# Retention and an exact-GELU MLP on one core: q and k turned as 2-byte values, one plane per feature of a pair

## The chip, the core and the metric

The kernel runs on one core of a Trainium2 chip. A core has TensorE (PE in the profile: matrix products; PEld is its weight load), VectorE (DVE), ScalarE (ACT), GpSimd (POOL), SyncE (SP) and 16 DMA engines. The metric is the device time of one execution in microseconds, the median of several runs. Inputs and the output are float32; the products inside run in bfloat16.

## The reference

```python
# q, k, v: (8 batches, 8 heads, 576 positions, 64 features)
scores = scale * np.matmul(q, k.transpose(0, 1, 3, 2))
gamma = 1.0 - 2.0 ** (-5.0 - np.arange(H, dtype=np.float32))
rel = pos[:, None] - pos[None, :]
Dmat = np.where(rel >= 0, gamma[:, None, None] ** rel[None, :, :], 0.0)
ret = scores * Dmat[None, :, :, :]
attn = np.matmul(ret, v)
# x: (4608 tokens, 512)
x = attn.transpose(0, 2, 1, 3).reshape(B * S, H * D)
h = x @ w_in                    # w_in: (512, 2048)
g = 0.5 * h * (1.0 + erf(h * inv_sqrt2))
out = g @ w_out                 # w_out: (2048, 512)
```

There is no softmax: scores are multiplied by a power of gamma that depends on the distance. That lets the sum over distant keys be kept as a state of 64 x 64 per head, so that only a block of 128 x 128 around the diagonal needs explicit scores.

## The kernel before

**Units and groups.** A unit is 128 positions of one batch, with all eight heads. The first four units are position block 0 of batches 0 to 3, each a group by itself ("raw" units). After them come groups of two units (two batches, the same block of positions); the last 64 positions of two batches form one short unit, a group of one. For a group the steps are: turn q and k so that features lie on partitions (T), scores (S, function `scores`), mask and copy out of PSUM (`masked`, line 628), product with v (`inner`), the state (`state`), the product of q with the state (`cross`), and the evacuation into x (`evacuate`, line 771). Four units fill one block of 512 tokens of x, of which there are nine; a block then goes through the MLP: `mlp1` or `mlp1_fast` with `w_in`, GELU on ScalarE, `mlp2` or `mlp2_fast` with `w_out`. The fast forms compute a product of 2 x 2 blocks with seven block products, for which VectorE makes sums of operands.

**How q and k are turned.** There are three ways. Units 0 to 3 and the two groups after them (`BY_PE`) are transposed by TensorE and copied out of PSUM. The other 16 groups (`BY_DVE`) are turned by VectorE, which transposes blocks of 32 x 32. For these, the load puts the data so that 32 partitions hold 32 blocks of t consecutive positions (t = 4 for a full unit, 2 for a short one), and each quarter of the partitions holds one combination of head parity and batch. A head has 64 features but a quarter has 32 partitions, so each partition holds two adjacent features, a pair. In the kernel before, `turn_dve` (line 550) reads the 2-byte data as 4-byte values, one value per pair, and so keeps the two features of a pair side by side. For k the products read the result with a step of two. For q a function `apart` (line 561) copies it on ScalarE into two halves, one for each feature of the pair, back into q's load buffer. Scores and `cross` run one product for each feature of the pair and add them up.

**Buffers.** Tiles are taken in rings with a tag: "lq" and "lk" hold loaded q and k, "tq" and "tk" turned ones, "kn" k in its plain layout, "v" and "vh" v and v scaled. A ring's tile is taken again once a condition given with it holds; `nT`, `nA` and `nB` count the groups turned and the units whose scores and whose product with v have been put out.

**The order of work.** All instructions are put out by a planner written in Python, which runs when the kernel is built. It keeps a clock `T` for each engine, adds a fixed duration to it for each instruction, notes when each load should land (`land`), and at each step of TensorE's clock picks what is due (the loop from line 1274). `fire` (line 1193) puts out the side work of the other engines. `AHEAD` and `RATE` bound how far the scores may run ahead of the MLP; `LEAD` says from which lead on two neighbouring groups do their products with v and the state together, `NEAR` how long MLP work holds back for that, `JOIN` allows scores right behind such a step. The order in which GpSimd puts out the first loads is a list, `ORDER`: q, k, v with the number of a unit, "wi" and "wo" eighths of `w_in` and `w_out`, "n" a plain copy of k, "dq" a step of the table of decays, and "io" the constants (line 187), which begin with two index ramps on GpSimd (lines 188 and 190); the identity for TensorE's transposes and the decay masks `near` follow from them on VectorE and ScalarE. Unit 0's q, k and v are loaded by SP's and ScalarE's queues as float32 and cast.

**Warm-up and fill.** TensorE begins with `N_WARM` products of 512 columns on a tile of zeros. Later, up to `WARM_TO`, the planner puts such products into gaps that it foresees (`warm`, line 1230). `HOT` is the time until which it counts a product at twice its duration.

The lines that turn and copy q, before:

```python
src = loaded[groups[n][0]][0][x][:, 0:2 * m].bitcast(FP32).rearrange("p (h t e) -> p h t e", h=HP, e=32)
dst = (turned(n, 1) if x else sg[n]["pairs"]).rearrange("p h s -> p (h s)")[:, 0:2 * m].bitcast(FP32)
nc.vector.transpose(dst.rearrange("p (h b t) -> p h t b", h=HP, b=32), src)
```

Of the kernel before, what the change touches and what calls it, by code (L numbers as in the profile page):

```python
# [9 lines left out]
FP32 = mybir.dt.float32  # L10
BF16 = mybir.dt.bfloat16
# [6 lines left out]
def kernel(  # L18
# [54 lines left out]
    BY_PE = range(4, 4 + NPE)  # L73
    BY_DVE = range(4 + NPE, N_G)
    raw = range(4)
    N_LQ = 6
    N_LK = 4
    N_TQ = 2
    N_TK = 4
    N_KN = 4  # L80
    VH_POOL = 16
    N_VH = 4
    VH_ACT = [4, 22, 1]
    N_XB = 4
    AHEAD = 13
    RATE = 4.6
    STORE_AT = 62.0
    CROWD = 66.0
    STATE10 = 32.0
    HOT = 7.5  # L90
    FETCH = 5.0
    ARRIVE = 5.6
    WPLUS = 0
    WARM_TO = 24.0
    JOIN = 0
    JOIN_SB = 0.0
    VISIT = 4
    LEAD = 5.0
    NEAR = 0.6
    SLACK, SB, PER_G, PER_B, TURN0 = 1.2, 2.0, 8.0, 20.0, 0.0  # L100
    FINE = 0.38
    FPOOL = 0.6
    N_V = 6
    MASK_ACT = 99.0
    V0_HW = 1
    N_WARM = 7
    MSK_AT = 24.0
    HK = N_DF // 2

    const = ctx.enter_context(tc.tile_pool(name="const", bufs=1))  # L110
# [156 lines left out]
    def tiles_of(i):  # L267
        g = groups[group_of[i]]
        if i not in loaded:
            if i < 4:  # L270
                loaded[i] = ([early_slice(2 * i + a, 1).rearrange("p (h d) -> p h d", h=H) for a in range(2)],
                             early_slice(8 + i, 1).rearrange("p (h d) -> p h d", h=H), None)
            else:
                n = group_of[i]
                if i != g[0]:
                    qk, v_, kn = loaded[i - 1]
                elif n in BY_PE:
                    qk = [ring("lq", [128, 2 * H * D], BF16, "q_ld", lambda: nB > g[-1]),
                          ring("lk", [128, 2 * H * D], BF16, "k_ld", lambda: all(y in s_done for y in g) and nT > n)]
                    kn = qk[1].rearrange("p (h j d) -> p j h d", j=2, h=H)  # L280
                else:
                    qk = [ring("lq", [128, 2 * H * D], BF16, "q_ld", lambda: nB > g[-1]),
                          ring("lk", [128, 2 * H * D], BF16, "k_ld", lambda: nT > n)]
# [97 lines left out]

    def next_order():
        item = ORDER.pop(0)
# [122 lines left out]
    def turned(n, x):  # L506

        s = sg[n].setdefault("turned", {})
        if n < 4:
            if not s:  # L510
                t = ring("kn", [128, 2, HP, 128], BF16, "qkT", lambda: nB > n)
                s[0], s[1] = t[:, 0], t[:, 1]
        elif x not in s:
            s[x] = ring("tk", [128, H, 128], BF16, "kT", lambda: nA > groups[n][-1])
        return s[x]

    def turn(n, jj):

        qk = loaded[groups[n][0]][0][jj]
        if n < 4:  # L520
            b, t = bank([128, HP, 128], BF16, "qk_ps")
            dst, m = turned(n, jj), HP
            for x in range(HP):
                mm_turn(t[:, x], qk[:, 2 * x:2 * x + 2, :], ident1)
        else:
            b, t = bank([128, H, 128], BF16, "qk_ps")
            dst, m = turned(n, 1) if jj else qk.rearrange("p (h s) -> p h s", h=H), H
            for y in range(2):
                for hp in range(HP):
                    mm_turn(t[:, y * HP + hp], qk[:, 4 * D * hp + y:4 * D * hp + 4 * D:2], ident1)  # L530
# [7 lines left out]
    apart_due = []  # L538

    def pairs_of(n):  # L540
        return HP * (TAIL if units[groups[n][0]][2] is None else C)

    def turn_dve(n, x):

        m = pairs_of(n)
        src = loaded[groups[n][0]][0][x][:, 0:2 * m].bitcast(FP32).rearrange("p (h t e) -> p h t e", h=HP, e=32)
        if x == 0:
            sg[n]["pairs"] = ring("tq", [128, H, 128], BF16, "qT", lambda: n not in [x[0] for x in apart_due])
        dst = (turned(n, 1) if x else sg[n]["pairs"]).rearrange("p h s -> p (h s)")[:, 0:2 * m].bitcast(FP32)
        nc.vector.transpose(dst.rearrange("p (h b t) -> p h t b", h=HP, b=32), src)  # L550
        done = on("dve", 0.13 + m / 530, max(land["qk"[x], i] for i in groups[n])) + SEM
        if x == 0:
            apart_due.append((n, done))
        else:
            sg[n]["T"] = max(sg[n].get("T", 0.0), done)

    def apart():

        n, ready = apart_due.pop(0)
        m = pairs_of(n)  # L560
        nc.scalar.copy(loaded[groups[n][0]][0][0][:, 0:2 * m].rearrange("p (y n) -> p y n", y=2),
                       sg[n]["pairs"].rearrange("p h s -> p (h s)")[:, 0:2 * m].rearrange("p (n y) -> p y n", y=2))
        sg[n]["T"] = max(sg[n].get("T", 0.0), on("act", 0.15 + m / 580, ready) + SEM)

    def turned_q(n, sl, hp, y):
        m = pairs_of(n)
        return loaded[groups[n][0]][0][0][sl, y * m + hp * m // HP:y * m + (hp + 1) * m // HP]

    def turned_k(n, sl, hp, y):
        m = pairs_of(n)  # L570
        if n in BY_PE:
            return turned(n, 1)[sl, y * HP + hp, :]
        return turned(n, 1)[sl].rearrange("p h s -> p (h s)")[:, 2 * hp * m // HP + y:2 * (hp + 1) * m // HP:2]

    def scores(n):
        g = groups[n]
# [9 lines left out]
        else:  # L586
            short = len(g) == 1
            got = [bank_pair(TAIL if short else C) for _ in g]
            for hp in range(HP):
                for y in range(2):  # L590
                    for e in range(2):
                        for j in range(2):
                            sl = slice(64 * e + 32 * j, 64 * e + 32 * j + 32)
                            dst = got[0][1][64 * j:64 * j + 64, e, hp, :] if short else got[j][1][:, e, hp, :]
                            mm(dst, lhsT=turned_k(n, sl, hp, y), rhs=turned_q(n, sl, hp, y),
                                             start=(y == 0), stop=(y == 1), skip_group_check=True)
            done = pe(0.25 if short else 0.42, "row4x2" if short else "row4")
            for j, i in enumerate(g):
# [136 lines left out]
    def cross(n):  # L735
# [6 lines left out]
        for hp in range(HP):  # L742
            for y in range(2):
                for e in range(2):
                    for j in range(2):
                        sl = slice(64 * e + 32 * j, 64 * e + 32 * j + 32)
                        mm(o[64 * e:64 * e + 64, j, hp, :], lhsT=u[sl, 2 * hp + y, :], rhs=turned_q(n, sl, hp, y),
                                         start=False, stop=(hp == HP - 1 and y == 1), skip_group_check=True)
        done = pe(0.25 if j0 is None else 0.4, "row4x2")
        for i in g:  # L750
# [442 lines left out]
    def fire():  # L1193
# [17 lines left out]
        while apart_due and apart_due[0][1] <= now + 0.1 and T["act"] <= now + (0.5 if apart_due[0][0] > group_of[min(nA, N_U - 1)] else 3.0):  # L1211
            apart()
        while True:
            jobs = side_jobs(now)
            if not jobs:
# [39 lines left out]
    def s_ready(early=0):  # L1255
        n = group_of[nA]
        g = groups[n]
        if n < nT and n not in [x[0] for x in apart_due] and g[-1] // 4 <= tM1 + N_XB - 1 and nA + len(g) <= AHEAD + early + RATE * b1:
            return sg[n]["T"]
        return 1e9  # L1260

# [7 lines left out]
    for _ in range(N_WARM):  # L1269
        b, t = bank([128, 512], FP32, "warm")  # L1270
        mm(t, lhsT=zeros[:, :128], rhs=zeros, start=True, stop=True)
        release(b, 0.0)
    T["pe"] = 1.3 + 0.62 * N_WARM
    while True:
        fire()
        now = T["pe"]
# [97 lines left out]
        if apart_due:  # L1374
            soon.append(max(apart_due[0][1], T["act"]) + 0.01)
        if wsum or sum_due:
            soon.append(T["dve"] + 0.01)
        if stores:
# [41 lines left out]
```

## Time and profile before

| | |
|---|---|
| median of 3 runs | 292.75 us (291.52 to 293.8) |
| span of the profiled execution | 288.7 us |
| granted TensorE clock in it | 1.000 |
| instructions | 9727 |
| DMA | 31.96 MB, mean 111 GB/s |

The span reaches from the first to the last instruction of the profiled execution. Busy times of an engine are unions of its instructions' durations; products overlap in the array, so a group's mean duration is longer than its share of the time. Rows of a group read: line, engine, operation, output and inputs, shape, count, then busy us and the mean ns of one, then idle time of the engine just before, and what ended it. Rows of the timeline read: start us, us, engine, line, operation, count, and in brackets the idle time before it. Rows by stage give the stretch, its length, then for each engine its busy time and count of instructions, the granted clock, DMA and GB/s.

### The profile page before, as it was taken

Reading aid. Unit: us, or ns where it says so; the run is one execution under the profiler, and the core shown is the slowest. Engines: PE = TensorE matmul, PEld = TensorE weight load, DVE = VectorE, ACT = ScalarE, POOL = GpSimd, SP = SyncE. Lnnn points to the kernel's source line nnn. Section 1 sums busy time; section 2 is a strip of 40 time slices with the busy share of each in tenths; the row PEclk is TensorE's granted clock in tenths of the full one; section 3 lists DMA queues with packets and bytes.
Section 4 is the critical chain, followed back from the end, with each engine's and each line's share of the span. In section 5 each row is a group of like instructions: output and inputs, shape, how many; then the busy total and the mean of one; then the engine's idle time right before and its main releaser. Section 6 shows DMA issues by size and latency. Waiting matters only on the chain.

```text
span 288.7 us, 9727 instructions
## 1 busy us (share of the span) xinstructions
PE 279.1 (97%) x4138; PEld 212.5 (74%) x4162; DVE 229.5 (80%) x384; ACT 178.8 (62%) x400; POOL 136.2 (47%) x205
## 2 busy tenths in 40 slices
PE   6899999999999999999999999999999999999994
PEld 2478767888667766666766766777888888888883
DVE  5564289897964799968996799897996998899861
ACT  7355537998378767778578866655645455555421
POOL 8956868996899777678688820000000000000000
PEclk9999999999999999999999999999999999999999
DMA  9999999999989999999999960302020202101114
GB/s 155 170 183 202 185 163 203 201 124 150 116 98 135 140 169 116 184 133 190 163 122 185 82 104 3 77 2 75 0 75 0 76 3 73 73 2 73 39 55 128
DMA packets 109131, 31.96 MB, mean 111 GB/s; under 512 B 85792, under 2 KB 104736, under 8 KB 109088
## 3 DMA queue, kind: packets, MB, share of 16 engines
q0 software_dynamic: 100400, 21.12, 83.2%
q1 hardware_dynamic: 7264, 9.51, 9.9%
q10 hardware_dynamic: 1424, 0.72, 0.9%
q8 instruction: 32, 0.52, 0.7%
q14 instruction: 11, 0.09, 0.1%
HBM read 42.99 MB, written 9.44 MB: 182 GB/s over the span
## 4 chain that ended last, share of the span: by engine, by line
PE 95%; DMA 2%; issue 1%; DVE 0%; POOL 0%; ACT 0%; POOLq 0%; DVEq 0%
PE psum L452 93%; DMA early<-in_q_dram 2%; PE psum L456 1%; POOL w_in L311 0%; DVE qkT L487 0%; DVE o_sb L884 0%; ACT t L489 0%; POOL val L188 0%; POOLq L188 0%; DVEq L487 0%; POOLq L1404 0%; POOL pos L190 0%
## 5 line engine op out<-in xcount | busy, mean ns | idle before, releaser
L452 PE MATMUL psum<-x,w_in 128*128 128x256 bf16 (+2 forms) x716 | 116.8, 303 | 1.6 <-issue 0.8
L452 PEld LDWEIGHTS <-w_in 128*128 128x128 bf16 x736 | 68.1, 98 | 26.1 <-issue 0.3
L452 PEld LDWEIGHTS <-g_all 128*128 128x128 bf16 x576 | 55.6, 98 | 15.1 <-issue 0.6
L452 PE MATMUL psum<-w_out,g_all 128*128 128x256 bf16 (+1 forms) x438 | 58.6, 280 | 0.0
L799 ACT ACTIVATE g_all<-psum 128x512 bf16<-128x512 f32 x64 | 37.7, 594 | 22.8 <-PE psum L452 22.5
L452 PEld LDWEIGHTS <-s 128*128 128x128 bf16 x408 | 39.3, 98 | 8.5
L346 POOL DMA_DIRECT2D k_ld<-in_k_dram x64 | 35.1, 566 | 18.1 <-DMA q_ld<-in_q_dram 10.3
L645 ACT ACTIVATE vh<-v_ld,dv 128x128 bf16<-128x128 bf16 (+1 forms) x144 | 42.2, 379 | 0.0
L628 DVE TENSOR_TENSOR ret<-psum,msk 128x1024 bf16<-128x1024 f32 (+1 forms) x32 | 35.6, 1150 | 7.3 <-PE psum L452 7.2
L1013 ACT ACTIVATE g_all<-t 128x512 bf16<-128x512 f32 x36 | 22.6, 630 | 29.0 <-DVE t L1021 28.9
L346 POOL DMA_DIRECT2D q_ld<-in_q_dram x64 | 35.3, 570 | 2.0 <-DMA v_ld<-in_v_dram 0.9
L452 PE MATMUL psum<-wt,s 128*128 128x256 bf16 x272 | 34.3, 273 | 0.0
L489 ACT COPY t<-psum 128x256 f32<-128x256 f32 (+1 forms) x46 | 20.0, 436 | 21.8 <-PE psum L452 21.5
L884 DVE TENSOR_TENSOR o_sb<-psum,t 128x256 f32<-128x256 f32 x51 | 21.4, 420 | 12.0 <-ACT t L489 6.3
L1021 DVE TENSOR_TENSOR t<-psum,t 128x512 f32<-128x512 f32 x36 | 24.7, 689 | 6.1 <-ACT t L489 4.2
L487 DVE COPY t<-psum 128x512 f32<-128x512 f32 (+1 forms) x41 | 22.6, 558 | 2.9 <-PE psum L452 2.9
L802 ACT ACTIVATE g_all<-psum 128x512 bf16<-128x512 f32 (+1 forms) x36 | 19.3, 549 | 8.0 <-PE psum L452 7.7
L771 DVE TENSOR_TENSOR x<-psum,dqT 128x1024 bf16<-128x1024 f32 (+1 forms) x18 | 19.4, 1095 | 1.1 <-PE psum L452 1.1
L452 PE MATMUL psum<-x,ws 128*128 128x256 bf16 x144 | 19.5, 273 | 0.0
L357 POOL DMA_DIRECT2D v_ld<-in_v_dram x14 | 16.3, 1167 | 4.0 <-ACT g_all L799 2.0
L452 PE MATMUL psum<-wt,g_all 128*128 128x256 bf16 x136 | 17.5, 273 | 0.5 <-ACT t L489 0.5
L452 PE MATMUL psum<-w_out,s 128*128 128x256 bf16 x136 | 17.5, 273 | 0.0
(100 smaller groups left out, 325.9 us busy)
## 6 DMA issues: line engine op xcount, KB each, us to landing
out_dram<-o_sb SPq DMA_DIRECT2D x31, 256.0 KB, 2.4
v_ld<-in_v_dram POOLq DMA_DIRECT2D x14, 256.0 KB, 5.5
q_ld<-in_q_dram POOLq DMA_DIRECT2D x48, 64.0 KB, 5.1
k_ld<-in_k_dram POOLq DMA_DIRECT2D x48, 64.0 KB, 4.5
kn_ld<-in_k_dram POOLq DMA_DIRECT2D x12, 256.0 KB, 6.1
w_in<-in_moe_w_in_dram POOLq DMA_DIRECT2D x8, 256.0 KB, 8.1
w_out<-in_moe_w_out_dram POOLq DMA_DIRECT2D x8, 256.0 KB, 9.5
k_ld<-in_k_dram POOLq DMA_DIRECT2D x4, 128.0 KB, 7.8
```

Source lines behind the costliest of these rows:

```text
L346: nc.gpsimd.dma_start(qk["qk".index(what)][p0:p0 + 32, 0:HP * per].rearrange("p (h x) -> p h x", h=HP), {"q": q, "k": k}[what][2 * bp + jj ...
L452: nc.tensor.matmul(*a, **k)
L487: nc.vector.tensor_copy(dst, src)
L489: nc.scalar.copy(dst, src)
L628: nc.vector.tensor_tensor(both.rearrange("p (e h) s -> p e h s", e=2), t, by, op=ALU.mult)
L645: nc.scalar.activation(vh[:, 0:m, h], src[:, :, h], AF.Copy, scale=dv[:, h, ci:ci + 1])
L771: nc.vector.tensor_tensor(x.rearrange("p m (j s) -> p j m s", j=2), o, by, op=ALU.mult)
L799: nc.scalar.activation(g_all[:, t % 2, :, m0, :], hT.rearrange("p n (a c) -> p (n a) c", a=2), AF.Gelu)
L802: nc.scalar.activation(g_of(t, 2 * lo // TOK)[:, m0:m0 + n, lo_:lo_ + hi - lo], hT, AF.Gelu)
L884: nc.vector.tensor_tensor(dst, src, f[key], op=ALU.add)
L1013: nc.scalar.activation(g_of(t, part)[:, m0:m0 + 2], src, AF.Gelu)
L1021: nc.vector.tensor_tensor(f[key], f["b"][1], f[key], op=ALU.add)
```

## The change

1. `turn_dve` transposes 2-byte values. Its output has, for each pair of heads, one plane for each feature of the pair. q is turned into a ring of its own ("tq"), as k is into "tk"; `apart` is gone with its conditions, and TensorE's transposes write the same order of planes. `turned_half` reads both q and k for the products. The planner's duration for a transpose stays as it was.
2. The ring "lq" has 4 tiles in place of 6, "tq" 4 in place of 2, and q's load buffer is free once q has been turned.
3. 12 warm-up products in place of 7, and other planned durations for products before `HOT`, with other rules for fill.
4. Another `ORDER`, other planned landing times for unit 0's q and k, and other values of `AHEAD`, `RATE`, `HOT`, `JOIN`, `LEAD`, `NEAR` and `MSK_AT`.

```diff
-    N_LQ = 6
+    N_LQ = 4
-    N_TQ = 2
+    N_TQ = 4
-    AHEAD = 13
-    RATE = 4.6
+    AHEAD = 15
+    RATE = 4.2
-    HOT = 7.5
+    HOT = 8.0
-    WPLUS = 0
-    JOIN = 0
+    JOIN = 2
-    LEAD = 5.0
-    NEAR = 0.6
+    LEAD = 3.0
+    NEAR = -0.4
-    N_WARM = 7
-    MSK_AT = 24.0
+    N_WARM = 12
+    MSK_AT = 22.0
...
-                    qk = [ring("lq", [128, 2 * H * D], BF16, "q_ld", lambda: nB > g[-1]),
+                    qk = [ring("lq", [128, 2 * H * D], BF16, "q_ld", lambda: nT > n or nT == n and half),
...
-    land["q", 0], land["k", 0] = 4.65, 5.2
+    land["q", 0], land["k", 0] = 5.05, 5.3
...
-    ORDER = ("wi0 io q1 k2 k1 wi7 v1 q2 k3 v0 wi1 wi6 q3 wo2 v2 wi5 v3 wi3 wi4 wo1 wi2 wo3 wo0 wo4 wo5 k4 q4 wo7 "
-             "q5 wo6 v4 dq2 k5 q6 k7 k6 q7 q8 q9 n4 v6 k8 k9 v8 q10 k11 n8 n6 k10 dq3 q11 q12 v10 dq0 q13 dq4 k12 "
-             "k13 n10 n12 v12").split()
+    ORDER = ("q1 k3 wi0 io k2 v1 v0 q2 wi7 k1 wi6 wo2 q3 wi1 v3 wi5 v2 wi3 wo0 wo3 wo4 wi2 wo1 wi4 k4 wo5 wo7 q4 "
+             "q5 k5 dq2 wo6 v4 q8 q6 k7 q7 n4 k6 v6 q9 n8 k9 k8 q10 n6 v8 k11 dq3 k10 n10 k12 q11 dq0 q12 v10 dq4 "
+             "q13 k13 n12 v12").split()
...
-            s[x] = ring("tk", [128, H, 128], BF16, "kT", lambda: nA > groups[n][-1])
+            if x:
+                s[x] = ring("tk", [128, H, 128], BF16, "kT", lambda: nA > groups[n][-1])
+            else:
+                s[x] = ring("tq", [128, H, 128], BF16, "qT", lambda: nB > groups[n][-1])
...
-        src = loaded[groups[n][0]][0][x][:, 0:2 * m].bitcast(FP32).rearrange("p (h t e) -> p h t e", h=HP, e=32)
...
-        nc.vector.transpose(dst.rearrange("p (h b t) -> p h t b", h=HP, b=32), src)
+        src = loaded[groups[n][0]][0][x][:, 0:2 * m].rearrange("p (h t e y) -> p h t y e", h=HP, y=2, e=32)
+        dst = turned(n, x).rearrange("p h s -> p (h s)")[:, 0:2 * m]
+        nc.vector.transpose(dst.rearrange("p (h y b t) -> p h t y b", h=HP, y=2, b=32), src)
...
-    def apart():
-
-        n, ready = apart_due.pop(0)
-        m = pairs_of(n)
-        nc.scalar.copy(loaded[groups[n][0]][0][0][:, 0:2 * m].rearrange("p (y n) -> p y n", y=2),
-                       sg[n]["pairs"].rearrange("p h s -> p (h s)")[:, 0:2 * m].rearrange("p (n y) -> p y n", y=2))
...
+    def turned_half(n, x, sl, hp, y):
+        w = pairs_of(n) // HP
+        return turned(n, x)[sl].rearrange("p h s -> p (h s)")[:, (2 * hp + y) * w:(2 * hp + y + 1) * w]
...
-                            mm(dst, lhsT=turned_k(n, sl, hp, y), rhs=turned_q(n, sl, hp, y),
+                            mm(dst, lhsT=turned_half(n, 1, sl, hp, y), rhs=turned_half(n, 0, sl, hp, y),
...
-        pe((0.32 if T["pe"] < HOT else 0.2158) * n)
+        pe(0.2158 * n)
...
-    T["pe"] = 1.3 + 0.62 * N_WARM
+    T["pe"] = 1.2 + 0.427 * N_WARM
...
-        if now < WARM_TO and gap > (0.6 if now < HOT else 0.2 if now < 16 else 0.5):
-            warm(int(gap / 0.6) + WPLUS if now < HOT else max(1, round(gap / 0.23)) + WPLUS)
+        if now < WARM_TO and gap > (0.45 if now < HOT else 0.25 if now < 16 else 0.5):
+            warm(int(gap / (0.45 if now < HOT else 0.23)))
```

More of the change, by code (lines that the diff above doesn't have):

```diff
@@ L281, in tiles_of @@
                 else:
-                    qk = [ring("lq", [128, 2 * H * D], BF16, "q_ld", lambda: nB > g[-1]),
+                    qk = [ring("lq", [128, 2 * H * D], BF16, "q_ld", lambda: nT > n or nT == n and half),
                           ring("lk", [128, 2 * H * D], BF16, "k_ld", lambda: nT > n)]
@@ L526, in turn @@
             b, t = bank([128, H, 128], BF16, "qk_ps")
[L527 to L530, printed above, removed]
+            dst, m = turned(n, jj), H
+            for hp in range(HP):
+                for y in range(2):
+                    mm_turn(t[:, 2 * hp + y], qk[:, 4 * D * hp + y:4 * D * hp + 4 * D:2], ident1)
         done = pe(0.056 * m)
@@ L534, in turn @@
         sg[n]["T"] = max(sg[n].get("T", 0.0), done + SEM)
-    apart_due = []
     def pairs_of(n):
@@ L545, in turn_dve @@
         m = pairs_of(n)
-        src = loaded[groups[n][0]][0][x][:, 0:2 * m].bitcast(FP32).rearrange("p (h t e) -> p h t e", h=HP, e=32)
[L547 to L550, printed above, removed]
-        done = on("dve", 0.13 + m / 530, max(land["qk"[x], i] for i in groups[n])) + SEM
[L552 to L555, printed above, removed]
-    def apart():
-        n, ready = apart_due.pop(0)
-        m = pairs_of(n)
-        nc.scalar.copy(loaded[groups[n][0]][0][0][:, 0:2 * m].rearrange("p (y n) -> p y n", y=2),
-                       sg[n]["pairs"].rearrange("p h s -> p (h s)")[:, 0:2 * m].rearrange("p (n y) -> p y n", y=2))
[L563 to L573, printed above, removed]
+        src = loaded[groups[n][0]][0][x][:, 0:2 * m].rearrange("p (h t e y) -> p h t y e", h=HP, y=2, e=32)
+        dst = turned(n, x).rearrange("p h s -> p (h s)")[:, 0:2 * m]
+        nc.vector.transpose(dst.rearrange("p (h y b t) -> p h t y b", h=HP, y=2, b=32), src)
+        done = on("dve", 0.13 + m / 530, max(land["qk"[x], i] for i in groups[n])) + SEM
+        sg[n]["T"] = max(sg[n].get("T", 0.0), done)
+    def turned_half(n, x, sl, hp, y):
+        w = pairs_of(n) // HP
+        return turned(n, x)[sl].rearrange("p h s -> p (h s)")[:, (2 * hp + y) * w:(2 * hp + y + 1) * w]
     def scores(n):
@@ L746, in cross @@
                         sl = slice(64 * e + 32 * j, 64 * e + 32 * j + 32)
-                        mm(o[64 * e:64 * e + 64, j, hp, :], lhsT=u[sl, 2 * hp + y, :], rhs=turned_q(n, sl, hp, y),
+                        mm(o[64 * e:64 * e + 64, j, hp, :], lhsT=u[sl, 2 * hp + y, :], rhs=turned_half(n, 0, sl, hp, y),
                                          start=False, stop=(hp == HP - 1 and y == 1), skip_group_check=True)
@@ L1210, in fire @@
             state_cast()
-        while apart_due and apart_due[0][1] <= now + 0.1 and T["act"] <= now + (0.5 if apart_due[0][0] > group_of[min(nA, N_U - 1)] else 3.0):
-            apart()
         while True:
@@ L1257, in s_ready @@
         g = groups[n]
-        if n < nT and n not in [x[0] for x in apart_due] and g[-1] // 4 <= tM1 + N_XB - 1 and nA + len(g) <= AHEAD + early + RATE * b1:
+        if n < nT and g[-1] // 4 <= tM1 + N_XB - 1 and nA + len(g) <= AHEAD + early + RATE * b1:
             return sg[n]["T"]
@@ L1373 @@
             soon.append(cast_u[0][0])
-        if apart_due:
-            soon.append(max(apart_due[0][1], T["act"]) + 0.01)
         if wsum or sum_due:
```

## The prediction

> **What bounds the kernel now.** I read the page's head and its chain of waits first, then the busy time by stage.
>
> ```profile
> span 288.7 us, 9727 instructions
> PE 279.1 (97%) x4138; PEld 212.5 (74%) x4162; DVE 229.5 (80%) x384; ACT 178.8 (62%) x400; POOL 136.2 (47%) x205
> ...
> PE 95%; DMA 2%; issue 1%; DVE 0%; POOL 0%; ACT 0%; POOLq 0%; DVEq 0%
> ```
>
> TensorE holds 95% of the chain that ended last. DVE and ACT hold none of it, so work taken from them shortens nothing unless it ends a wait of TensorE. The same by stage (length, then busy time of PE, PEld, DVE, ACT and POOL), and below it the share of that which goes to products on `zeros`, the warm-up and fill work:
>
> ```profile
> 0.00:13.04 13.04, 9.85 (x56) 4.08 (x58) 7.34 (x34) 7.86 (x19) 11.91 (x20) 1.00 1.52 159
> 13.04:24.00 10.96, 10.54 (x186) 7.78 (x187) 7.80 (x13) 5.44 (x11) 7.10 (x10) 1.00 1.67 188
> 24.00:48.00 24.00, 23.36 (x274) 17.93 (x273) 13.92 (x24) 13.71 (x29) 18.19 (x24) 1.00 1.76 191
> 48.00:100.00 52.00, 51.56 (x1141) 38.98 (x1145) 41.00 (x54) 39.44 (x95) 45.35 (x71) 1.00 1.47 140
> 100.00:140.00 40.00, 39.63 (x707) 26.97 (x715) 35.85 (x48) 29.98 (x72) 31.27 (x48) 1.00 1.47 156
> 140.00:186.00 46.00, 45.42 (x766) 31.43 (x772) 39.56 (x56) 33.38 (x82) 22.36 (x36) 1.00 0.97 105
> 186.00:284.94 98.94, 98.69 (x1020) 85.32 (x1019) 83.65 (x157) 49.02 (x95) 0.00 (x0) 1.00 0.12 44
> 284.94:288.70 3.76, 0.00 (x0) 0.00 (x0) 0.42 (x1) 0.00 (x0) 0.00 (x0) 0.99 0.47 144
> ```
> ```profile
> 0.00:13.04 13.04, 7.09 (x16) 2.13 (x17) 0.27 (x1) 1.00 1.52 159
> 13.04:24.00 10.96, 2.30 (x9) 0.75 (x9) 0.00 (x0) 1.00 1.67 188
> ```
>
> From 24 us to 284.94 us TensorE is idle for 0.64 + 0.44 + 0.37 + 0.58 + 0.25 = 2.3 us of 261. Before 24 us it is idle for 3.6 us and runs 7.09 + 2.30 = 9.4 us of products that compute nothing. So 13 us are lost at the start, 3.76 us in the last store, and about 2 us in all the rest. The change can save time almost only before 24 us; it can lose it anywhere, if it makes TensorE wait.
>
> **The change, part by part.** *The transposes.* Each of 16 groups has q and k turned by VectorE as 4-byte pairs, and its q is then taken apart by ScalarE. The change turns twice as many 2-byte elements and drops the copy.
>
> ```profile
> L550 DVE STREAM_TRANSPOSE qT<-q_ld 128x512 f32<-128x512 f32 x12 | 13.3, 1107 | 0.0
> L550 DVE STREAM_TRANSPOSE kT<-k_ld 128x512 f32<-128x512 f32 x12 | 13.2, 1104 | 0.0
> ...
> L550 DVE STREAM_TRANSPOSE qT<-q_ld 128x256 f32<-128x256 f32 x4 | 1.7, 436 | 0.0
> L550 DVE STREAM_TRANSPOSE kT<-k_ld 128x256 f32<-128x256 f32 x4 | 1.7, 426 | 0.0
> ```
> ```profile
> L628 DVE TENSOR_TENSOR ret<-psum,msk 128x1024 bf16<-128x1024 f32 x28 | 32.9, 1217 | 7.3 <-PE psum L452 7.2
> ...
> L866 DVE TENSOR_TENSOR s<-g_all 128x1024 bf16<-128x1024 bf16 x17 | 11.5, 679 | 0.0
> ...
> L628 DVE TENSOR_TENSOR ret<-psum,msk 128x512 bf16<-128x512 f32 x4 | 2.6, 681 | 0.0
> ```
>
> No 2-byte transpose stands in this trace. The mask rows give the price of one element at a time: (1217 - 681) / 512 = 1.05 ns each and 145 ns fixed. By that measure the short 4-byte transposes run at (431 - 145) / 256 = 1.1 ns an element and the long ones at (1106 - 145) / 512 = 1.9 ns. What differs is the write step: t is 4 in the long form and 2 in the short one, so the long one writes every 16 bytes and the short one every 8. The new long form writes 2-byte elements with t = 4, every 8 bytes, as the short form does now. I therefore take 1.05 ns: 1.22 us for 1024 elements and 0.68 us for 512. That adds 24 x (1.217 - 1.106) + 8 x (0.681 - 0.431) = 2.7 + 2.0 = 4.7 us to VectorE. Bounds: two elements at a time, as the 679 ns row does, would give 24 x (0.679 - 1.106) + 8 x (0.41 - 0.431), a relief of 10.4 us (0.41 as 145 + 256 x 1.05 ns); 1.9 ns for every element would give 24 x (2.09 - 1.106) + 8 x (1.12 - 0.431), a burden of 29 us. What hides the 4.7 us is VectorE's idle time between 48 and 186 us, 11.0 + 4.2 + 6.4 = 21.6 us by the stages. Cost on the path: 0; with the cover gone, see the third rival.
>
> The Trainium skill (Advanced Engine Details and Errata, SBUF Cachelines) says that an access wants at least two hits on a 16-byte line and that another line at each access is slower. The 1.9 and 1.1 ns agree with it, and by it the new form stays unpunished, so the sum by the rule is the same 4.7 us and the bound of 29 us falls away.
>
> *The copy apart.* It goes:
>
> ```profile
> L561 ACT COPY q_ld<-qT 128x1024 bf16<-128x1024 bf16 (+1 forms) x16 | 15.0, 936 | 0.1
> ```
> ```profile
> PE psum L452 <- ACT t L489: 0.5, 1, 0.5
> ```
>
> ScalarE loses 15.0 of 178.8 us. TensorE waited once, for 0.5 us, for a ScalarE result after the start. I take -0.3 us, between 0 and -0.5. The tiles change too: q's load buffer comes free when it is turned, not when its last product is done, with 4 load and 4 turned buffers in place of 6 and 2. That lets loads start earlier on a queue that has nothing left after 186 us (POOL 0.00), so it is worth 0. The turned k is read without a step of two by the weight load; weight loads overlap products (PEld 74%), so 0.
>
> *The start.* Three loads now stand ahead of the two index ramps on GpSimd's queue, where one stood, and twelve warm-up products ahead of the first transpose, where seven stood.
>
> ```profile
> 1.25 0.90 POOL L311 DMA_DIRECT2D w_in<-in_moe_w_in_dram  x1 [0.80 <-POOLq L1404]
> 2.23 0.27 POOL L188 IOTA val<- 128x128 f32 x1
> ...
> 2.52 0.94 POOL L368 DMA_DIRECT2D early<-in_q_dram  x1
> 3.46 1.76 POOL L368 DMA_DIRECT2D early<-in_k_dram  x2
> ...
> 7.83 0.91 POOL L368 DMA_DIRECT2D early<-in_k_dram  x1
> ```
> ```profile
> 1.19 3.17 PE L452 MATMUL psum<-zeros 128*128 128x512 bf16 x7 [1.19 <-DVE zeros L151]
> 5.52 1.04 PE L456 MATMUL psum<-ident,early 128*128 128x128 bf16 x8 [1.16 <-DVE early L487]
> ...
> 8.77 2.77 PE L452 MATMUL psum<-zeros 128*128 128x512 bf16 x6
> 11.47 0.62 PE L452 MATMUL psum<-ret,early 128*32 128x128 bf16 x16
> 12.02 0.45 PE L456 MATMUL psum<-ident,early 128*128 128x128 bf16 x4
> ...
> 13.37 0.62 PE L452 MATMUL psum<-x,w_in 128*128 128x128 bf16 x8
> 13.83 1.03 PE L452 MATMUL psum<-zeros 128*128 128x512 bf16 x4
> ```
> ```profile
> 2.54 0.23 DVE L193 TENSOR_SCALAR far<-val 128x128 f32<-128x128 f32 x1 [0.59 <-POOL val L188]
> ...
> 3.85 0.16 DVE L209 TENSOR_TENSOR off<-lgT,pos 128x4 f32<-128x4 f32 x1
> 4.65 0.82 DVE L487 CAST early<-q 128x512 bf16<-128x512 f32 x1 [0.65 <-DMA q<-in_q_dram]
> 5.39 0.41 DVE L487 CAST early<-k 128x512 bf16<-128x512 f32 x1
> ...
> 8.04 1.27 DVE L623 TENSOR_TENSOR ret<-psum,near 128x512 bf16<-128x512 f32 x2
> ```
>
> The two extra loads cost 0.94 + 0.88 = 1.8 us of queue, so val starts at about 4.05 and not 2.23. VectorE's chain behind it, far to off, takes 4.01 - 2.54 = 1.5 us and ends at 5.8; the casts of q and k stand behind it on VectorE (0.74 from start to start, then 0.41) and end at 7.0, where they ended at 5.80. That is 1.2 us later. Against it: products of 512 columns take about 0.45 us each in the rows at 1.19 and 8.77 (3.17 / 7, 2.77 / 6) and 0.26 in the row at 13.83 (1.03 / 4). The granted clock stands at 1.00 in every stage, so the column doesn't show this; the change of speed falls between 11.5 and 13.8 us, 2.8 to 5.0 us into a stretch that began at about 8.8. Twelve products in a row from 1.19 us last at most 5.4 us, to 6.6, and should bring that change by 4 to 6 us. They end inside the wait for the casts. From the end of the k cast to unit 0's masked scores it took 9.31 - 5.80 = 3.5 us; the eight transposes in it, 1.04 us, would save some 0.5 at the higher speed, so the scores are done at 7.0 + 3.0 = 10.0. The first product that reads them began at 11.47, though they were ready at 9.31: six fill products stood ahead of it. Without them it begins at 10.1, 1.4 us earlier. With six, at 0.26 us each, or with the speed not risen, it begins between 11.5 and 12.7, up to 1.2 us later. I take -1.0 us, nearer the end that both the speed and the fill speak for.
>
> *The other loads.* Unit 1's k is the 4th load now, issued at about 4.4 us, and becomes the 8th, a place whose load goes out at 7.83. Loads of this kind landed a median 5.8 us after issue:
>
> ```profile
> early<-in_k_dram POOLq DMA_DIRECT2D x3, 128.0 KB, 5.8
> ```
>
> That is 7.83 + 5.8 = 13.6 us, where TensorE turned it at 12.02, so unit 1 can be 1.6 us late, and the units are taken in order. What covers it: unit 0's products with the pieces of w_in that have landed, and the 2.30 us of fill after 13.04, which say that TensorE had slack there. All q and k of the four first units are in by the 11th load as before. The last piece of w_in goes from the 19th load to the 22nd, and while it is missing TensorE has the other 14 of the 16 chunks of w_in to work on. I take 0, with bounds of -2.3 (all of the later fill goes) and +1.6.
>
> *Order and pairs.* LEAD, NEAR, JOIN, AHEAD and RATE say when attention steps are put between MLP products and when two groups go together. Every change of tile shape and every refill of instructions costs TensorE some time, of which the profile shows "issue", 1% of the chain, 2.9 us. A third of it either way is the bound; looser rules for pairs make fewer changes, so I take -0.3 us.
>
> Sum: -0.3 - 1.0 + 0 - 0.3 = -1.6 us, 288.7 to 287.1 us of span. The median of the runs is 292.75, 4.05 us above this span, and I carry that over: 291.1 us, 0.5% faster. A measurement of this kernel tells about 1% from no change.
>
> **The rivals.** *The start gains more.* The full 1.4 us, all 2.30 us of later fill, and 0.6 us from pairs and ScalarE: -4.3 us, 288.4 us. For it: all that fill is time in which only inputs were missing, and the first q is loaded first now. Against it: k of unit 1 and w_in come later.
>
> *The constants come too late.* Slower: everything at the start hangs on val, 1.8 us later, through the identity that the transposes need, and unit 1's k adds its 1.6 us: +3.4 us, 296.2 us. It decides if the casts on VectorE stay behind the chain of constants and the fill products still stand ahead of unit 0. For it: the chain before 24 us has no branch around val. Against it: the 2.2 us between 9.31 and 11.47.
>
> *VectorE becomes the bound.* Slower: at 1.9 ns an element VectorE gets 29 us more between 48 and 186 us, and has 21.6 us idle there; TensorE waits for the rest, 7.5 us, 300.2 us at most, less where work can be put off behind 186 us, where 15.3 us are idle. It decides at 1.6 ns an element, about 1.8 us for a long transpose. For it: that is what the 1106 ns row gives per element.
> The Trainium skill (VectorE: DVE Perf Modes, The TRN2 errata) says that 2-byte data taken as 4-byte elements halve VectorE's time, which would make the new form twice the old, 2.2 us; the two 4-byte rates above speak against it.
>
> *Nothing moves.* Start and loads cancel: 292.7 us.
>
> **How the numbers follow.** Forecast 0.41, more gain at the start 0.29, nothing 0.08, constants too late 0.13, VectorE 0.09. The range is 287 to 296.5: it holds the gain with the uncertainty of its fill on one side and the late constants on the other, and leaves out most of the VectorE case and the far edge of the gain. Faster by over 1% (under 289.8): the second case and little of the first, 0.31. Slower by over 1% (over 295.7): the two slow cases, 0.22. Within 1%: 0.47.
>
> **What would show it.** The transpose rows: long ones near 1.22 us, short ones near 0.68, no copy row on ScalarE, and VectorE's idle time at its transposes unchanged at 0. The first products on w_in near 12.4 us rather than 13.37, with the 512-column products at under 0.3 us before 7 us. Less fill between 13 and 24 us. TensorE busy to within 2 to 3 us from 24 us to its end. I am wrong if long transposes take over 1.8 us, if unit 0's first transposes wait past 7.5 us and its first products on w_in start after 13.4, or if TensorE shows new waits on qT, kT or loads between 24 and 186 us.

## The result, and the profile after

The changed kernel takes 309.22 us (308.38 to 309.72, 4 runs) against 292.13 us before: a ratio of 1.061, with a 95% interval from 1.057 to 1.065. It is 6.1% slower. The forecast of 291.1 us was wrong, and so was the upper end of its range, 296.5.

The page of the changed kernel, first the busy times, then the chain of waits by engine and by line:

```profile
span 307.6 us, 9671 instructions
PE 284.7 (93%) x4151; PEld 212.8 (69%) x4151; DVE 258.9 (84%) x380; ACT 167.0 (54%) x386; POOL 136.2 (44%) x205
...
PE 62%; DVE 16%; POOL 8%; DMA 7%; issue 3%; ACT 2%; DVEq 0%; POOLq 0%
PE psum L451 62%; DVE kT L548 5%; DMA w_in<-in_moe_w_in_dram 3%; DVE qT L548 3%; POOL early L367 3%; DMA kn_ld<-in_k_dram 2%; DMA q_ld<-in_q_dram 2%; DVE ret L609 1%; ACT vh L626 1%; DVE s L847 1%; POOL w_in L310 1%; DVE o_sb L865 1%; DVE x L752 1%; POOL k_ld L345 1%; POOL q_ld L345 1%
```

TensorE's share of the chain fell from 95% to 62%, and VectorE's rose from nothing to 16%, half of it in the two transposes of line 548. Busy time by stage shows where TensorE lost it (columns as in the prediction):

```profile
24.00:48.00 24.00, 24.00 (x341) 18.08 (x342) 13.35 (x24) 12.74 (x26) 17.74 (x24) 1.00 1.85 184
48.00:100.00 52.00, 46.27 (x906) 34.26 (x904) 48.08 (x47) 30.97 (x78) 44.53 (x69) 0.97 1.34 132
100.00:140.00 40.00, 37.56 (x575) 25.02 (x573) 34.45 (x38) 23.91 (x64) 25.65 (x39) 1.00 1.33 135
140.00:186.00 46.00, 39.77 (x750) 26.67 (x749) 45.68 (x46) 25.90 (x68) 28.99 (x46) 1.00 1.12 112
```

From 48 to 186 us TensorE is idle for 5.7 + 2.4 + 6.2 = 14.4 us; it was 1.4 us before. VectorE is busy for 45.68 of the 46 us of the last of these stages. Over the whole span, TensorE's idle time rose by 13.3 us (307.6 - 284.7 against 288.7 - 279.1) and its busy time by 5.6. The groups of VectorE, and TensorE's waits after that (engine and line, what it waited for: us in total, times, longest):

```profile
L548 DVE STREAM_TRANSPOSE qT<-q_ld 128x1024 bf16<-128x1024 bf16 x12 | 29.6, 2466 | 0.0
L548 DVE STREAM_TRANSPOSE kT<-k_ld 128x1024 bf16<-128x1024 bf16 x12 | 29.5, 2458 | 0.0
...
L548 DVE STREAM_TRANSPOSE qT<-q_ld 128x512 bf16<-128x512 bf16 x4 | 3.0, 743 | 0.0
L548 DVE STREAM_TRANSPOSE kT<-k_ld 128x512 bf16<-128x512 bf16 x4 | 3.0, 738 | 0.0
```
```profile
PE psum L451 <- DVE kT L548: 12.7, 7, 2.4
```

A long transpose takes 2.46 us where it took 1.11, a short one 0.74 where it took 0.43. That is 24 x 1.356 + 8 x 0.310 = 35.0 us more of transposes on VectorE (its busy time as a whole rose by 29.4 us). And seven waits for turned k, 12.7 us in all, nearly make up TensorE's 13.3 us of added idle time. One of them in the timeline:

```profile
67.24 1.04 PE L451 MATMUL psum<-wt,g_all 128*128 128x256 bf16 x8
67.39 2.47 DVE L548 STREAM_TRANSPOSE kT<-k_ld 128x1024 bf16<-128x1024 bf16 x1
...
69.92 0.62 PE L451 MATMUL psum<-qT,kT 32*128 32x128 bf16 x32 [1.65 <-DVE kT L548]
...
70.48 1.05 PE L451 MATMUL psum<-x,w_in 128*128 128x256 bf16 x8
```

The transpose began at 67.39 and would have been done by 68.5 at the duration that the planner counts. TensorE's eight products ended at 68.27, and the scores stand next in its queue. The MLP products behind them, which need nothing of the transpose, could only start after the scores.

### The profile page after: what moved, and what is told of

It reads as the page before. It is cut to its first block, busy times and chain, and to the rows that moved or that the text cites. A ratio compares the mean times of both kernels' runs of the same rounds, so it can differ in the third digit from the quotient of the medians.

```text
span 307.6 us, 9671 instructions
## 1 busy us (share of the span) xinstructions
PE 284.7 (93%) x4151; PEld 212.8 (69%) x4151; DVE 258.9 (84%) x380; ACT 167.0 (54%) x386; POOL 136.2 (44%) x205
## 4 chain that ended last, share of the span: by engine, by line
PE 62%; DVE 16%; POOL 8%; DMA 7%; issue 3%; ACT 2%; DVEq 0%; POOLq 0%
PE psum L451 62%; DVE kT L548 5%; DMA w_in<-in_moe_w_in_dram 3%; DVE qT L548 3%; POOL early L367 3%; DMA kn_ld<-in_k_dram 2%; DMA q_ld<-in_q_dram 2%; DVE ret L609 1%; ACT vh L626 1%; DVE s L847 1%; POOL w_in L310 1%; DVE o_sb L865 1%; DVE x L752 1%; POOL k_ld L345 1%; POOL q_ld L345 1%
## 5 line engine op out<-in xcount | busy, mean ns | idle before, releaser
L451 PE MATMUL psum<-x,w_in 128*128 128x256 bf16 (+2 forms) x720 | 121.2, 310 | 2.4 <-DMA w_in<-in_moe_w_in_dram 1.5
L451 PE MATMUL psum<-w_out,g_all 128*128 128x256 bf16 (+1 forms) x440 | 59.3, 280 | 0.2 <-DVE u_sb L692 0.2
L548 DVE STREAM_TRANSPOSE qT<-q_ld 128x1024 bf16<-128x1024 bf16 (+1 forms) x16 | 32.6, 2035 | 0.0
L548 DVE STREAM_TRANSPOSE kT<-k_ld 128x1024 bf16<-128x1024 bf16 (+1 forms) x16 | 32.4, 2028 | 0.0
L451 PE MATMUL psum<-qT,kT 32*128 32x128 bf16 (+1 forms) x576 | 11.1, 210 | 13.0 <-DVE kT L548 12.7
L451 PEld LDWEIGHTS <-kT 32*128 32x128 bf16 (+1 forms) x576 | 7.9, 96 | 18.2 <-DVE kT L548 15.1
```

Source lines behind the costliest of these rows:

```text
L451: nc.tensor.matmul(*a, **k)
L548: nc.vector.transpose(dst.rearrange("p (h y b t) -> p h t y b", h=HP, y=2, b=32), src)
```

## The experiments

**One part of the change at a time.** First the transposes alone: the kernel before with the 2-byte transposes, their rings and no copy apart.

```diff
-    N_LQ = 6
+    N_LQ = 4
-    N_TQ = 2
+    N_TQ = 4
...
-        nc.vector.transpose(dst.rearrange("p (h b t) -> p h t b", h=HP, b=32), src)
+        nc.vector.transpose(dst.rearrange("p (h y b t) -> p h t y b", h=HP, y=2, b=32), src)
```

> The kernel before with nothing but the 2-byte transposes, their buffers and no copy apart; its own load order, warm-up and planning values stay. Theory (VectorE's time): a long transpose takes 2.46 us in place of 1.11 and a short one 0.74 in place of 0.43, so VectorE gets 35 us more between 48 and 200 us, and the time rises by 12 to 18 us over the kernel before, with TensorE waiting for turned k for over 10 us. Rival (load order, warm-up and planning values cost the time): within 4 us of the kernel before.

Measured: 313.49 us, a ratio of 1.076 (1.071 to 1.081), about 4 us beyond the expected range and far from the rival's. The wait for kT is less than the 10 us expected, but the mask step behind it is late too:

```profile
PE psum L452 <- DVE kT L549: 7.8, 8, 1.9
PE psum L452 <- DVE ret L610: 5.1, 5, 2.5
```

Then everything else alone: the load order, the warm-up, the fill rule and the planning values, with the 4-byte transposes and the copy of before.

```diff
-    AHEAD = 13
+    AHEAD = 15
-    N_WARM = 7
+    N_WARM = 12
...
-    ORDER = ("wi0 io q1 k2 k1 wi7 v1 q2 k3 v0 wi1 wi6 q3 wo2 v2 wi5 v3 wi3 wi4 wo1 wi2 wo3 wo0 wo4 wo5 k4 q4 wo7 "
+    ORDER = ("q1 k3 wi0 io k2 v1 v0 q2 wi7 k1 wi6 wo2 q3 wi1 v3 wi5 v2 wi3 wo0 wo3 wo4 wi2 wo1 wi4 k4 wo5 wo7 q4 "
```

> The kernel before with the new load order, the 12 warm-up products, the new fill rule and planning values; q and k are turned as 4-byte pairs and copied apart as before. Theory (VectorE's time): within 3 us of the kernel before. Rival (load order, warm-up and planning values): 10 to 17 us slower than it.

Measured: 291.55 us, ratio 1.000 (0.997 to 1.002). The whole loss belongs to the transposes. The other values neither gain nor lose with fast transposes, though the changed kernel with them is faster (1.061) than the transposes alone with the old ones (1.076).

**The write step.** The same kernel, written side by side:

```diff
-        nc.vector.transpose(dst.rearrange("p (h y b t) -> p h t y b", h=HP, y=2, b=32), src)
+        nc.vector.transpose(dst.rearrange("p (h y t b) -> p h t y b", h=HP, y=2, b=32), src)
```

> The changed kernel, but VectorE writes the turned values one beside the other: the positions of a unit come out in the order of t, then block, and meet the mask and v in that order, so the output is not the reference's. Theory (the write step makes the transposes slow, and their time makes the kernel slow): long transposes 1.2 us, short ones 0.68, kernel 288 to 294 us. Rival 1 (2-byte elements or the read with a step of two are slow): long transposes stay at 2.4 us and the kernel at 306 to 311 us. Rival 2 (the rest of the change costs the time): transposes 1.2 us, kernel above 300 us.

Measured: 292.25 us, ratio 1.002 (1.000 to 1.005). Its transposes in the groups of VectorE:

```profile
L548 DVE STREAM_TRANSPOSE qT<-q_ld 128x1024 bf16<-128x1024 bf16 x12 | 14.8, 1233 | 0.0
L548 DVE STREAM_TRANSPOSE kT<-k_ld 128x1024 bf16<-128x1024 bf16 x12 | 14.6, 1218 | 0.0
L548 DVE STREAM_TRANSPOSE qT<-q_ld 128x512 bf16<-128x512 bf16 x4 | 2.8, 700 | 0.0
L548 DVE STREAM_TRANSPOSE kT<-k_ld 128x512 bf16<-128x512 bf16 x4 | 2.8, 693 | 0.0
```

These are close to the 1.22 and 0.68 us of the prediction. The number of elements, their size and the read with a step of two are the same as in the changed kernel; only the write step differs. So it is the write step of four 2-byte elements that doubles the long transposes, and that alone carries 5.9 of the 6.1%.

**The cost of a write step by itself.** Two runs held only transposes, of 1024 2-byte or 512 4-byte elements in a partition.

> Transposes alone, six of each form one after the other, on 2-byte (b) and 4-byte (f) elements, with the number of elements and the write step (s) in the name, reads side by side; then the changed kernel's two forms, and those with dense writes. The output is zeros. Theory 1 (a write step of 4 elements is slow, whatever their size): b1024s1 and s2 about 1.2 us, b1024s4 about 2.4, f512s1 and s2 about 0.68, f512s4 1.1. Theory 2 (only a write step of 16 bytes is slow): b1024s4 1.2 us, b1024s8 slow, f512s4 slow. Theory 3 (the read with a step of two is what is slow): b1024s4 1.2 us, and both the new long form and the dense long form 2.4 us.

In this run the forms came out interleaved and the profile joins names that differ in a number, so most of its rows mix steps. Its unmixed rows gave 2.40 us for the new long form, against theory 2, and 1.18 for the long form written side by side, against theory 3. It was repeated in a fixed order with other names:

```python
for step in (1, 2, 4, 8, 16):
    nc.vector.transpose(d[:, 0:n].rearrange("p (g b t) -> p g t b", b=32, t=step),
                        s[:, 0:n].rearrange("p (g t e) -> p g t e", e=32, t=step))
```

> Transposes alone in a fixed order, four of each: 1024 elements of two bytes and 512 of four bytes, reads side by side, write steps of 1, 2, 4, 8 and 16 elements; at the end 1024 two-byte elements read with a step of two and written side by side. The output is zeros. Theory 1 (a step of 4 elements or more costs, by elements): two-byte 1.2, 1.2, 2.4 us, four-byte 0.66, 0.66, 1.02 for steps 1, 2 and 4, and the same factor from 8 on. Theory 2 (2-byte writes cost by the step in their own way): two-byte step 8 near 4.7 us, twice step 4, while four-byte steps 4 to 16 stay near 1.0. The read with a step of two costs nothing: 1.2 us.

The groups of VectorE in that run (the first letter of one name is cut):

```profile
L28 DVE STREAM_TRANSPOSE twobyte_step_eight<-src 128x1024 bf16<-128x1024 bf16 x4 | 18.8, 4708 | 0.1
L28 DVE STREAM_TRANSPOSE twobyte_step_sixteen<-src 128x1024 bf16<-128x1024 bf16 x4 | 18.0, 4496 | 0.1
L28 DVE STREAM_TRANSPOSE twobyte_step_four<-src 128x1024 bf16<-128x1024 bf16 x4 | 9.7, 2430 | 0.1
L28 DVE STREAM_TRANSPOSE twobyte_step_two<-src 128x1024 bf16<-128x1024 bf16 x4 | 5.2, 1295 | 0.1
L28 DVE STREAM_TRANSPOSE twobyte_step_one<-src 128x1024 bf16<-128x1024 bf16 x4 | 5.0, 1245 | 0.1
L34 DVE STREAM_TRANSPOSE ead_step_two_write_dense<-src 128x1024 bf16<-128x1024 bf16 x4 | 4.9, 1233 | 0.1
L28 DVE STREAM_TRANSPOSE fourbyte_step_eight<-src 128x512 f32<-128x512 f32 x4 | 4.4, 1091 | 0.1
L28 DVE STREAM_TRANSPOSE fourbyte_step_four<-src 128x512 f32<-128x512 f32 x4 | 4.3, 1069 | 0.1
L28 DVE STREAM_TRANSPOSE fourbyte_step_sixteen<-src 128x512 f32<-128x512 f32 x4 | 4.1, 1028 | 0.1
L28 DVE STREAM_TRANSPOSE fourbyte_step_one<-src 128x512 f32<-128x512 f32 x4 | 3.0, 750 | 0.1
L28 DVE STREAM_TRANSPOSE fourbyte_step_two<-src 128x512 f32<-128x512 f32 x4 | 2.8, 701 | 0.1
```

Up to a step of two both sizes run within 7% of the time that they take side by side. With 2-byte elements a step of 4 costs a factor of about 2 and one of 8 about 4, and then it stays. With 4-byte elements a step of 4 or more costs a factor of about 1.5 and no more. That is theory 2 of this run, and of theory 1 only the first three figures for each size.

**Time or order?** The planner still counts 1.10 us for a long transpose. With its true duration:

```diff
-        done = on("dve", 0.13 + m / 530, max(land["qk"[x], i] for i in groups[n])) + SEM
+        done = on("dve", 2.46 if m == HP * C else 0.74, max(land["qk"[x], i] for i in groups[n])) + SEM
```

> The changed kernel, whose planner counts 2.46 us for a long transpose and 0.74 for a short one, as measured, in place of 1.10 and 0.61. Theory 1 (VectorE has too little free time between 48 and 200 us, whatever the order): at most 5 us of the 17 come back, 303 to 310 us. Theory 2 (the fixed order is planned on a wrong duration, and steps that could run meanwhile stand behind the wait): more than half comes back, 293 to 300 us.

Measured: 295.77 us, ratio 1.018 (1.016 to 1.020). Of 6.1%, 4.3 come back, as theory 2 said, with the same slow transposes:

```profile
L548 DVE STREAM_TRANSPOSE qT<-q_ld 128x1024 bf16<-128x1024 bf16 x12 | 29.7, 2475 | 0.0
```
```profile
PE psum L451 <- ACT t L488: 2.1, 2, 1.6
PE psum L451 <- DVE x L752: 1.4, 1, 1.4
```

Above, one row of its transposes, then TensorE's two longest entries in the list of waits. No wait for kT is left. What remained of the loss was parted by one more run, in which the instructions stand in this order but VectorE writes side by side.

> The planner counts 2.46 and 0.74 us for the transposes, so all instructions stand in the order of the run with true durations, but VectorE writes side by side and needs 1.2 and 0.7 us; the positions meet the mask and v in another order, so the output is not the reference's. It parts what is left of the loss there, 295.8 against 291.1 us. Theory 1 (VectorE's own 30 us cost it, where it has no free time left): 292 us or less. Theory 2 (the order that is planned around a slow VectorE costs it): 294 to 296 us.

Measured: 293.83 us, ratio 1.010 (1.007 to 1.013), just below the range of theory 2 and above that of theory 1. Of the 1.8%, about 1.0 lies in the order made for slow transposes and 0.8 in VectorE's time itself; the two intervals leave some 0.4 either way.

**Half the dose.** The changed kernel with q in the new form and k as 4-byte pairs:

```diff
-        nc.vector.transpose(dst.rearrange("p (h y b t) -> p h t y b", h=HP, y=2, b=32), src)
+        if x:
+            nc.vector.transpose(dst.bitcast(FP32).rearrange("p (h b t) -> p h t b", h=HP, b=32),
+                                raw_.bitcast(FP32).rearrange("p (h t e) -> p h t e", h=HP, e=32))
+        else:
+            nc.vector.transpose(dst.rearrange("p (h y b t) -> p h t y b", h=HP, y=2, b=32),
+                                raw_.rearrange("p (h t e y) -> p h t y e", h=HP, y=2, e=32))
```

> The changed kernel, with q turned in the new form and k as 4-byte pairs as before, read with a step of two: half of the slow transposes, 17 us more on VectorE in place of 35, which its 21.6 us of idle time in the stages from 48 to 186 us could hold. Theory 1 (free time of VectorE decides, with a threshold): within 3 us of the kernel before. Theory 2 (each slow transpose costs its share, by the wait behind it): 7 to 10 us slower than the kernel before.

Measured: 296.48 us, ratio 1.020 (1.019 to 1.022): 5 us or so, between both theories. Its waits:

```profile
PE psum L451 <- DVE kT L549: 3.5, 6, 1.0
```

There is no threshold at which VectorE's free time is used up: six waits of at most 1.0 us appear, although its idle time would have held the 17 us. But half the dose costs a third, not half. The waits average 0.6 us where they averaged 1.8. That fits a result that is late by the overrun of one transpose in place of two, k being turned after q, with part of the lateness covered by work that already stands in TensorE's queue; this reading was not tested further.

**The start.** The warm-up alone, and the load order alone, on the kernel before:

```diff
-    N_WARM = 7
+    N_WARM = 12
...
-    T["pe"] = 1.3 + 0.62 * N_WARM
+    T["pe"] = 1.2 + 0.427 * N_WARM
```

> The kernel before with 12 warm-up products and the new durations and rules of fill alone; load order, planning values and transposes as before. Theory (the start gains 1 to 1.4 us, and the later load of w_in takes it away in the changed kernel): 0.5 to 1.5 us faster than the kernel before. Rival (what comes in early waits for loads in any case): within 0.5 us.

```diff
-    land["q", 0], land["k", 0] = 4.65, 5.2
+    land["q", 0], land["k", 0] = 5.05, 5.3
```

> The kernel before with the new load order and the two planned landing times that go with it; warm-up, planning values and transposes as before. Theory (the first piece of w_in and the constants come later): 0.5 to 2 us slower than the kernel before. Rival (loads have slack): within 0.5 us.

Measured: 291.00 us for the warm-up, ratio 1.000 (0.997 to 1.003), and 291.77 us for the load order, 1.005 (1.003 to 1.006). The warm-up did what was expected of it at first, as TensorE's timeline in that run shows; the second fence is a later stretch of it:

```profile
10.75 0.41 PE L452 MATMUL psum<-ret,early 128*32 128x128 bf16 x16
...
11.85 0.61 PE L452 MATMUL psum<-x,w_in 128*128 128x128 bf16 x8
```
```profile
38.08 3.63 PE L452 MATMUL psum<-w_out,g_all 128*128 128x512 bf16 x20
```

The first products on w_in come at 11.85 us, 1.5 us before those of the kernel before. The same stretch in the kernel before:

```profile
38.44 3.63 PE L452 MATMUL psum<-w_out,g_all 128*128 128x512 bf16 x20
```

So 0.36 us of the 1.5 are left at that point, and in the end no gain that the interval, 0.8 us either way, could show. Work that is brought forward at the start runs into inputs that have not come: TensorE's waits for loads of q and v in this run are 1.7 + 0.4 us, where it waited 0.7 us before. The load order alone costs 0.5%, about 1.3 us. In its timeline 12 fill products stand ahead of the first products on w_in, which come 0.4 us later than before:

```profile
11.16 2.76 PE L452 MATMUL psum<-zeros 128*128 128x512 bf16 x12
13.76 0.61 PE L452 MATMUL psum<-x,w_in 128*128 128x128 bf16 x8
```

**A version that might beat both.** q written side by side and read by the products with a step of 32 columns, in natural order; k as 4-byte pairs, read with a step of two as before. Once with the old order and values, once with the new.

```diff
-        return turned(n, x)[sl].rearrange("p h s -> p (h s)")[:, (2 * hp + y) * w:(2 * hp + y + 1) * w]
+        flat = turned(n, x)[sl].rearrange("p h s -> p (h s)")
...
+        if x:
+            return flat[:, 2 * hp * w + y:2 * (hp + 1) * w:2]
+        return flat[:, (2 * hp + y) * w:(2 * hp + y + 1) * w].rearrange("p (t b) -> p b t", b=32)
```

> A version that could beat both, with the output of the reference: q is turned as 2-byte values written side by side, and the products read it with a step of 32 columns in natural order; k as 4-byte pairs, read with a step of two. No copy apart. Load order, warm-up and planning values as in the kernel before. Theory (TensorE is the bound and neither engine's relief ends a wait): 0 to 1 us from the kernel before, with q's transposes at 1.2 us. Rival 1 (the products read slowly with that step): the 32-row products take longer than 215 ns and the kernel is 3 us or more slower. Rival 2 (15 us less on ScalarE helps): 1.5 us or more faster.

> The same q and k with the load order, warm-up and planning values of the changed kernel. Theory: within 1 us of the kernel before, like the run with these values alone. Rivals as in the run before.

Measured: 324.67 and 323.59 us, ratios 1.113 (1.108 to 1.118) and 1.111 (1.108 to 1.114). TensorE's products of scores (`kT`) and of q with the state (`u_sb`), first in the kernel before, then in the run with the old order:

```profile
L452 PE MATMUL psum<-q_ld,kT 32*128 32x128 bf16 x448 | 8.8, 215 | 0.0
...
L452 PE MATMUL psum<-q_ld,u_sb 32*64 32x128 bf16 x384 | 7.2, 216 | 0.0
```
```profile
L452 PE MATMUL psum<-qT,kT 32*128 32x128 bf16 x448 | 24.1, 364 | 0.0
...
L452 PE MATMUL psum<-qT,u_sb 32*64 32x128 bf16 x384 | 19.8, 359 | 0.0
```

The transposes are fast here, but the same number of score products keeps TensorE busy for 24.1 us in place of 8.8, and the products with the state for 19.8 in place of 7.2. These 27.9 us are most of the 33 that the run is slower. That is rival 1: moving the step from VectorE's write to TensorE's read moves the cost to the engine that bounds the kernel. No version tried is faster than the kernel before by more than the runs scatter.

## Why the prediction was wrong, point by point

**What bounds the kernel: right.** TensorE was the bound and only a new wait of it could cost much. That is what came, and it can be seen in one row, the 12.7 us for kT. The prediction had named both among its signs of being wrong: transposes over 1.8 us, and new waits on kT.

**The price of a 2-byte transpose: this step failed.** I took 1.05 ns an element from the mask rows and reasoned that a write every 8 bytes would run as the short 4-byte form does. Measured were 2.46 us for the long form, even more than the bound of 2.09 that I had set from the long 4-byte form. The two 4-byte forms differed in two ways, a step of 16 against 8 bytes and of 4 against 2 elements. I read the difference as one of bytes; for 2-byte elements the element count was the safer reading, as the row twobyte_step_four shows. The short form, with t = 2, came out at 0.74 us, near the 0.68 forecast; in the run that writes side by side the long form came out at its forecast too, 1.22 to 1.23.

The Trainium skill (Advanced Engine Details and Errata, SBUF Cachelines) wants two hits on a 16-byte line, which a step of 8 bytes gives. The 4-byte rows agree: 701 ns at that step, 1069 at 16 bytes. The 2-byte rows don't: 2430 ns at a step of 8 bytes against 1245 side by side. The measurement decides, and the bound of 29 us that the prediction let fall by this rule was passed, at 35. The Trainium skill's other rule, that 2-byte data taken as 4-byte halve VectorE's time (VectorE: DVE Perf Modes, The TRN2 errata), which the prediction set aside, came near for the long forms, 2.46 against 1.11 us. But side by side the factor is 1.6, 1.23 to 0.75; the rest is the write step, which costs the 2-byte form more.

**The cover: wrong as well.** The third rival, with a chance of 0.09, had the right cause, slow transposes for which TensorE waits, but priced it wrongly. It let VectorE's idle time of 21.6 us hold the first part of the burden and gave 7.5 us at most; the loss was 17 us. TensorE waited though VectorE was not full: by the stages, VectorE still had 3.9 + 5.6 + 0.3 = 9.8 us idle between 48 and 186 us. TensorE's order is fixed when the kernel is built, on planned durations, and a result that is due at a fixed place in its queue and comes later makes it wait, whatever idle time VectorE has elsewhere. With true durations in the plan the 35 us cost 1.8%, about 5 us, which is below that rival's own figure.

**The copy apart: right.** It hid behind TensorE. With transposes side by side and no copy the kernel is at 1.002, so 15 us less on ScalarE were worth nothing. The -0.3 us taken is less than these runs can tell.

**The start: near at its place, in part by luck, and worth nothing measurable at the end.** The first product that reads unit 0's masked scores began at 9.71 us in the changed kernel (forecast 10.1, before 11.47):

```profile
8.31 1.47 PE L451 MATMUL psum<-zeros 128*128 128x512 bf16 x6
9.71 0.52 PE L451 MATMUL psum<-ret,early 128*32 128x128 bf16 x16
...
13.12 0.62 PE L451 MATMUL psum<-x,w_in 128*128 128x128 bf16 x8 [0.84 <-DMA w_in<-in_moe_w_in_dram]
```

Six fill products still stood ahead of it, a case that the prediction had put at 11.5 to 12.7. They took 0.25 us each and ran while VectorE was still making the masked scores, from 8.49 us for 1.29, so they cost almost nothing. And the first products on w_in came at 13.12, not 12.4, behind a wait for the first piece of w_in, which had gone from first to third in GpSimd's queue. I had counted the two loads ahead of the constants and not the same two ahead of w_in, whose last piece alone I followed. The warm-up run shows that the -1.0 us would hardly have reached the end in any case. The load order was given 0 and cost 1.3 us by itself, inside its bound of +1.6. Warm-up, load order and values together were given -1.0 + 0 - 0.3 us and measured 1.000.

## What to carry to other kernels

In these runs a VectorE transpose was fast when it wrote with a step of at most two elements. Where a step must be, 4-byte pairs carried it more cheaply than 2-byte values, and shifting the step into TensorE's reads of q cost far more. In a kernel whose order is fixed from planned durations, measure an instruction's duration in its exact access pattern before the plan counts on it: here a wrong duration made a loss of 1.8% into one of 6.1%.

## What the runs showed of the hardware

How the cost of the write step depends on the element size was not expected. By itself a transpose took, for 2-byte elements, 1.25, 1.30, 2.43, 4.71 and 4.50 us at steps of 1, 2, 4, 8 and 16 elements, and for half as many 4-byte elements 0.75, 0.70, 1.07, 1.09 and 1.03. What in the write path makes 2-byte elements suffer more was not tried.

The granted clock also dropped once in the changed kernel, after the wait shown above at 69.92 us and two more, of 1.7 to 1.9 us each, within 21 us. Three products of 512 columns right behind the last of them take 0.43 us each:

```profile
90.00:100.00 10.00, 9.29 (x164) 5.75 (x165) 7.33 (x10) 3.94 (x11) 9.26 (x15) 0.83 1.39 156
```
```profile
78.27 0.85 PE L451 MATMUL psum<-qT,kT 32*128 32x128 bf16 x32 [1.77 <-DVE kT L548]
...
90.70 0.63 PE L451 MATMUL psum<-qT,kT 32*128 32x128 bf16 x32 [1.89 <-DVE kT L548]
...
91.26 1.29 PE L451 MATMUL psum<-x,w_in 128*128 128x512 bf16 x3
```

At 0.83 of the clock over 10 us this is, by estimate, at most 1.7 us of TensorE's added 5.6 us of busy time. Another 0.7 is fill (products on `zeros` keep TensorE busy for 10.1 us in place of 9.4); the rest is not accounted for. Whether the waits brought the drop about was not tested, but such waits are not needed for one: in the run with q side by side and the old order, the clock was 0.56 from 68 to 70 us and 0.59 from 70 to 72, with TensorE busy for 3.91 of these 4 us and no wait of TensorE for a transpose in the whole run. What lowers the clock stays open.
